# Two sines of a rotation table moved between the copies of the first drive, and the imaginary rotation put first in each quarter

## The chip, the cores and the metric

One core of one Trainium2 chip. The metric is the device time of one execution in microseconds (us), of the slowest (here the only) core. Every number of the profile is from one execution with the hardware profiler on; its clock starts at the core's first instruction, and its span is some 1.8 us shorter than the device time of the same execution.

## The reference, cut to what matters

The input is 2048 tokens of 448 values. They are normalised, pass through a diagonal complex recurrence over the tokens and, beside it, through a gated feed-forward network; the two results are multiplied.

```python
xn = _layernorm(x)
Bu = jnp.einsum("bld,pd->blp", xn + 0j, B_bar)      # the "drive"
h = zeros
for t in range(L):
    h = Lam_bar[None, :] * h + Bu[:, t, :]          # 448 complex states
y = 2.0 * einsum("blp,dp->bld", hseq, Cmat).real + xn * Dskip
g = silu((silu(xn @ w_gate) * (xn @ w_up)) @ w_down)
out = x + y * g
```

## The kernel before

The tokens go in four quarters of 512. The complex recurrence is turned into two real ones: the drive is rotated by tables of cosines and sines (CT, ST), two real scans run, and the states are rotated back. The 448 states lie in four blocks of partitions; the last is a half block, whose real and imaginary parts are packed together. So the real rotation works on four blocks (KT = 4) and the imaginary one on three (KF = 3), plus the packed block once it has been turned over.

A table takes four instructions on VectorE (`table_phase`) and then two sines on ScalarE (`table_sin`). `params_trig` is one more small sine. The drive of a quarter is computed in two groups of four PSUM banks (PSUM is the memory that TensorE's matmuls write into); ScalarE copies each group out. The matmuls of gate and up for the next quarter take the same banks in turn.

```python
def bu(q, ns, packed=False):
    ...
    for two in (ns[:2], ns[2:]):                    # two groups of two blocks
        ...
        sums(q, pairs)                              # TensorE, 4 banks
        for n, pair in zip(two, pairs):
            for i in range(2):
                ...
                nc.scalar.activation(to, pair[i][0], ACT.Copy)
    if packed:
        turn_over(b1[:, KF, :], b0[:, KF, :])       # ScalarE
...
def drive(q, budget):
    bu_alloc(q)
    bu(q, (0, 1, 2), True)
    ...
    ssm_steps(bg, q)                                # rotation, scans, rotation back
    bg.run(budget)
...
gu(0, bg, 0.0, {                                    # first quarter's gate and up, with hooks
    ...
    4: [*transposes(4, 5, 6, 7), on(load_rest), on(table_phase, 1)],
    5: [on(table_sin, 1), on(table_phase, 2)],
    6: [on(table_sin, 2), on(table_phase, 3), on(params_fold), on(table_sin, 3),
        on(params_trig)],
}, ...)
drive(0, 0.0)
```

Each engine works through its own instructions in this order. On ScalarE the sines of the last table therefore stand ahead of the first copy of the first drive. In the profile, PE names TensorE, ACT ScalarE, DVE VectorE; the drive's output is `pb`, gate and up are `gp` and `up`, the down-projection is `hd`.

Of the kernel before, what the change touches and what calls it, by code (L numbers as in the profile page):

```python
# [10 lines left out]
ALU = mybir.AluOpType  # L11
# [33 lines left out]
def kernel(  # L45
# [22 lines left out]
    KF = D // P  # L68
# [23 lines left out]
    def block(n):  # L92
        return slice(n * P, (n + 1) * P)
# [13 lines left out]
    def ctile(shape, dtype, name):  # L107
        return const.tile(shape, dtype, name=name)

    def bank(name, dtype=F32):  # L110

        return psum.tile([P, 2048 // mybir.dt.size(dtype)], dtype, name=name, tag="bank")
# [10 lines left out]
    CT = ctile([P, KT, W], BF16, "CT")  # L123
    ST = ctile([P, KT, W], BF16, "ST")
# [214 lines left out]
    def params_out():  # L339
        tt, ts = nc.vector.tensor_tensor, nc.vector.tensor_scalar  # L340
        ab = pcol[:, 0:KT, 1:3].rearrange("p k c -> p c k")
        tt(out=lam[:], in0=lam[:], in1=rcol[:].unsqueeze(1).to_broadcast([P, 3, KT]),
           op=ALU.mult)
        ts(out=lam[:, 1, :], in0=lam[:, 1, :], scalar1=1.0, scalar2=None, op0=ALU.subtract)
        tt(out=prod[:, 0:2, :], in0=lam[:, 1:3, :], in1=ab, op=ALU.mult)
        tt(out=nb[:, 0, :], in0=prod[:, 0, :], in1=prod[:, 1, :], op=ALU.add)
        tt(out=prod[:, 0:2, :], in0=lam[:, 0:2, :], in1=ab, op=ALU.mult)
        tt(out=nb[:, 1, :], in0=prod[:, 0, :], in1=prod[:, 1, :], op=ALU.subtract)
        tt(out=b_re[:], in0=nb[:, 0, :], in1=rden[:], op=ALU.mult)
        tt(out=b_im[:], in0=nb[:, 1, :], in1=rden[:], op=ALU.mult)  # L350
        ts(out=nb_im[:], in0=b_im[:], scalar1=-1.0, scalar2=None, op0=ALU.mult)
# [42 lines left out]
    def bu_alloc(q):  # L394
        bu_of[q] = [
            work.tile([P, KT, W], BF16, name=f"bu_{c}") for c in ("re", "im")
        ]
# [10 lines left out]
    def sums(q, pairs, between=None):  # L408



        left = []
        for share, first in ((0, True), (1, False)):
            for n, two in enumerate(pairs):
                for m in range(4 - share):
                    for half in range(2):
                        out, w, (c0, c1) = two[half ^ share]
                        d, h = HALVES[half ^ share][share][m]
                        mm = nc.tensor.matmul(  # L419
                            out, lhsT=w[h, d, :], rhs=xT[h, d, q * W + c0 : q * W + c1],  # L420
                            start=(first and m == 0), stop=(not first and m == 3 - share),
                        )
                        if not first and m == 0:
                            told_of(mm, left[n])
                if first:
                    left.append(tell(mm))
            if first:
                run_power()
            if first and between:
                between()  # L430

    def bu(q, ns, packed=False):

        C1 = W // 2
        b0, b1 = bu_of[q]
        ns = [*ns, KF] if packed else ns
        for two in (ns[:2], ns[2:]):
            pairs = []
            for n in two:
                pb = [bank("pb") for _ in range(2)]  # L440
                if n < KF:
                    pairs.append([(pb[i][:], BT[:, :, block(m)], (0, W))
                                  for i, m in enumerate((n, KT + n))])
                else:
                    pairs.append([(pb[i][:, 0:C1], BT[:, :, block(KF)], (i * C1, i * C1 + C1))
                                  for i in range(2)])
            if pairs:
                sums(q, pairs)
            for n, pair in zip(two, pairs):
                for i in range(2):  # L450
                    to = bu_of[q][i][:, n, :] if n < KF else b0[:, KF, i * C1 : i * C1 + C1]
                    nc.scalar.activation(to, pair[i][0], ACT.Copy)  # L452
        if packed:
            turn_over(b1[:, KF, :], b0[:, KF, :])

    def turn_over(out, in_):

        for a, b in ((slice(0, R), slice(R, P)), (slice(R, P), slice(0, R))):
            nc.scalar.activation(out[a], in_[b], ACT.Copy)
# [3 lines left out]
    def ssm_steps(bg, q):  # L463
        T = {}

        def alloc():
            T["b"] = bu_of[q]
            T["e"] = [work.tile([P, KT - c, W], BF16, name=n, bufs=1)
                      for c, n in enumerate(("ere", "eim"))]
            T["t"] = work.tile([P, KT, W], BF16, name="tmp", bufs=1)  # L470
            T["h"] = H_of[q] = [work.tile([P, KT - c, W], BF16, name=n)
                                for c, n in enumerate(("H_re", "H_im"))]

        def of(z, n):
            z = T["t"] if z == "t" else T[z[0]][z[1]] if isinstance(z, tuple) else z
            return z[:, 0:n, :]

        def step(n, out, a, b, op):
            def run():
                if not T:  # L480
                    alloc()
                nc.vector.tensor_tensor(out=of(out, n), in0=of(a, n), in1=of(b, n), op=op)

            bg.add(q, 0.3 * n, run)

        def scan(k, c):
            init = 0.0 if q == 0 else H_of[q - 1][c][:, k, W - 1 : W]
            nc.vector.tensor_tensor_scan(  # L488
                out=T["b"][c][:, k, :], data0=rcol[:, k : k + 1].to_broadcast([P, W]),
                data1=T["e"][c][:, k, :], initial=init, op0=ALU.mult, op1=ALU.add,  # L490
            )

        b0, b1, e0, e1, h0, h1 = (z for n in "beh" for z in ((n, 0), (n, 1)))
        step(KT, e0, b0, CT, ALU.mult)
        step(KT, "t", b1, ST, ALU.mult)
        step(KT, e0, e0, "t", ALU.add)
        step(KF, e1, b1, CT, ALU.mult)
        step(KF, "t", b0, ST, ALU.mult)
        step(KF, e1, e1, "t", ALU.subtract)
        for k in range(KF, -1, -1):  # L500
            for c in range(2 if k < KF else 1):
                bg.add(q, 1.22, lambda k=k, c=c: scan(k, c))
        bg.add(q, 0.0, lambda: turn_over(T["b"][1][:, KF, :], T["b"][0][:, KF, :]))
        step(KF, h1, b1, CT, ALU.mult)
        step(KF, "t", b0, ST, ALU.mult)
        step(KF, h1, h1, "t", ALU.add)
        step(KT, h0, b0, CT, ALU.mult)
        step(KT, "t", b1, ST, ALU.mult)
        step(KT, h0, h0, "t", ALU.subtract)
# [88 lines left out]
    def on(fn, *args):  # L598
        return lambda: fn(*args)
# [56 lines left out]

    def drive(q, budget):
        bu_alloc(q)
        bu(q, (0, 1, 2), True)
        if q == 0:  # L660
            params_out()
        ssm_steps(bg, q)
        bg.run(budget)
# [16 lines left out]
    def do(fns):  # L680
        for fn in fns:
# [5 lines left out]
        3: norms(4, 5, 6, 7),  # L687
        4: [*transposes(4, 5, 6, 7), on(load_rest), on(table_phase, 1)],
        5: [on(table_sin, 1), on(table_phase, 2)],
        6: [on(table_sin, 2), on(table_phase, 3), on(params_fold), on(table_sin, 3),  # L690
            on(params_trig)],
    }, {0: first_pair, 1: second_pair})
    drive(0, 0.0)
    def cw(k):
        return [on(c_weights, k, nc.scalar)], [on(c_weights, k, nc.vector)]

    gu(1, bg, 2.2, {2: cw(0)[0], 3: cw(0)[1], 4: cw(1)[0], 5: cw(1)[1]})
    drive(1, 4.0)
    sg = downs(0, 1.2, {
        0: cw(2)[0] + cw(3)[0],  # L700
# [5 lines left out]
    outs(0, sg, {1: norms(10, 11) + transposes(10, 11)})  # L706
    sg = downs(1, 2.5)
    drive(2, 4.8)
    gu(2, bg, 1.6, {
        0: stats(12, 13),  # L710
# [47 lines left out]
```

## Time and profile before

| | before |
|---|---|
| median of the first 4 runs | 188.25 us (188.13 to 188.58) |
| the profiled execution | 189.09 us, span 187.2 us |
| PE / DVE / ACT busy | 97% / 85% / 55% |
| x of tokens 512 to 1023 landed | 14.08 us |
| last matmul pair of the first drive | starts at 35.33 us |
| first down-projection | starts at 63.05 us |

Starts to two decimals are those of the single instructions in the trace.

Its lines are in the prediction below.

### The profile page before, as it was taken

The page shows a single profiled execution, that of the slowest core. Times are in us where ns is not written, and L with a number is a line of the kernel's source. Part 1 is how long each engine was busy: PE and PEld are TensorE (multiplying, and loading weights), DVE is VectorE, ACT ScalarE, POOL GpSimd, SP SyncE. Part 2 cuts the span into 40 slices and gives each one's busy share as a digit, 9 for nine tenths or more (in the row PEclk, how much of TensorE's full clock was granted, in tenths as well). Part 3 has the DMA queues.
Part 4 walks back from the last instruction along what each step waited for, and adds up shares of the span by engine and source line. Part 5 has one row for each costly group of instructions (what it writes and reads, how often), then busy time and mean ns, then how long its engine had stood idle before and what let it go on. Part 6 is the DMA issues. An engine that isn't in the chain of part 4 may idle for free.

```text
span 187.2 us, 3749 instructions
## 1 busy us (share of the span) xinstructions
PE 181.0 (97%) x1493; PEld 92.4 (49%) x1493; DVE 159.9 (85%) x259; ACT 102.4 (55%) x197; POOL 12.6 (7%) x21
## 2 busy tenths in 40 slices
PE   7899999999999999999999999999999999999991
PEld 3574444455555655555454444555454444555561
DVE  4649799988999999999999999999939999996343
ACT  3236879898897972012289675301578757602110
POOL 7332200000000000400000400000000000000000
PEclk9999999999999999999999999999999999999999
DMA  5899694997000000152000041020000000011020
GB/s 169 212 279 328 111 116 96 160 294 276 0 4 0 5 0 0 27 119 67 0 0 5 0 84 32 0 83 15 2 4 0 4 0 0 4 51 49 0 74 25
DMA packets 25985, 12.59 MB, mean 67 GB/s; under 512 B 15984, under 2 KB 25968, under 8 KB 25968
## 3 DMA queue, kind: packets, MB, share of 16 engines
q1 hardware_dynamic: 24752, 11.95, 25.1%
q10 hardware_dynamic: 1088, 0.41, 0.8%
q8 instruction: 11, 0.18, 0.4%
q14 instruction: 6, 0.05, 0.1%
q0 software_dynamic: 128, 0.00, 0.0%
HBM read 7.11 MB, written 1.84 MB: 48 GB/s over the span
## 4 chain that ended last, share of the span: by engine, by line
PE 78%; DVE 10%; DMA 5%; SPq 2%; ACT 1%; issue 1%; POOL 1%; DVEq 0%
PE hd L558 23%; PE gp L419 18%; PE up L419 16%; PE y L573 11%; PE pb L419 9%; DMA x_all<-in_A_x_dram 3%; DMA Wg<-in_B_w_gate_dram 2%; DVE Vt L550 2%; PE y L579 2%; DVE f L363 2%; DVE st L236 1%; DVE xn L251 1%; DVE a L364 1%; DVE a L360 1%; DVE f L359 1%
## 5 line engine op out<-in xcount | busy, mean ns | idle before, releaser
L419 PE MATMUL gp<-xT,Wg 64*128 64x512 bf16 (+1 forms) x413 | 86.0, 365 | 0.7 <-ACT bu_re L452 0.3
L419 PE MATMUL up<-xT,Wu 64*128 64x512 bf16 (+1 forms) x413 | 85.5, 365 | 0.2
L419 PEld LDWEIGHTS <-Wg 64*128 64x128 bf16 x413 | 37.9, 94 | 23.5 <-issue 1.0
L419 PEld LDWEIGHTS <-Wu 64*128 64x128 bf16 x413 | 37.8, 94 | 20.7 <-issue 0.8
L558 PE MATMUL hd<-Wd,Vt 128*128 128x448 bf16 x224 | 43.2, 352 | 0.0
L542 ACT ACTIVATE gs<-gp 128x512 bf16<-128x512 f32 x56 | 33.8, 605 | 16.8 <-PE gp L419 16.7
L563 ACT ACTIVATE sg<-hd 128x448 bf16<-128x448 f32 x16 | 8.7, 544 | 49.0 <-PE hd L558 48.8
L546 ACT ACTIVATE us<-up 128x512 bf16<-128x512 f32 x54 | 33.0, 610 | 0.0
L558 PEld LDWEIGHTS <-Vt 128*128 128x128 bf16 x224 | 21.8, 98 | 20.5 <-issue 0.2
L419 PE MATMUL pb<-xT,BT 64*128 64x512 bf16 (+1 forms) x224 | 22.1, 349 | 0.0
L550 DVE TENSOR_TENSOR Vt<-gs,us 128x2048 bf16<-128x2048 bf16 (+1 forms) x16 | 17.3, 1081 | 0.9 <-ACT us L546 0.9
L573 PE MATMUL y<-C,H_re 128*128 128x448 bf16 (+2 forms) x68 | 17.6, 342 | 0.0
L589 DVE TENSOR_TENSOR t<-y,sg 128x448 f32<-128x448 f32 (+2 forms) x17 | 10.1, 595 | 8.3 <-PE y L573 7.4
L419 PEld LDWEIGHTS <-BT 64*128 64x128 bf16 x224 | 11.5, 94 | 10.8 <-issue 0.7
L488 DVE TENSOR_TENSOR_SCAN bu_re<-rcol,H_re,ere 128x512 bf16<-128x512 f32 x12 | 15.0, 1265 | 0.0
L579 PE MATMUL y<-Dd,xT 128*128 128x128 bf16 x64 | 13.5, 212 | 0.0
L222 POOL TENSOR_TENSOR rstd<-vep,halves 128x1 f32<-128x1 f32 (+1 forms) x7 | 7.2, 1023 | 86.5 <-DVE vep L238 58.0
L452 ACT ACTIVATE bu_re<-pb 128x512 bf16<-128x512 f32 (+1 forms) x20 | 9.9, 521 | 5.1 <-PE pb L419 5.1
L573 PE MATMUL y<-C,H_im 128*128 128x448 bf16 (+2 forms) x51 | 11.9, 342 | 0.0
L236 DVE BATCH_NORM_STATS2 st<-x_all 128x6 f32<-128x448 bf16 x16 | 9.9, 621 | 2.2 <-DMA x_all<-in_A_x_dram 2.1
L488 DVE TENSOR_TENSOR_SCAN bu_im<-rcol,H_im,eim 128x512 bf16<-128x512 f32 x9 | 11.4, 1262 | 0.0
L592 DVE TENSOR_TENSOR ob<-t,x_all 128x448 bf16<-128x448 f32 (+2 forms) x17 | 10.2, 597 | 0.6
(86 smaller groups left out, 159.7 us busy)
## 6 DMA issues: line engine op xcount, KB each, us to landing
out_dram<-ob SPq DMA_DIRECT2D x15, 112.0 KB, 1.7
Wd<-in_B_w_down_dram SPq DMA_DIRECT2D x1, 1568.0 KB, 9.7
x_all<-in_A_x_dram SPq DMA_DIRECT2D x1, 896.0 KB, 6.3
Wg<-in_B_w_gate_dram SPq DMA_DIRECT2D x2, 384.0 KB, 6.8
Wu<-in_B_w_up_dram SPq DMA_DIRECT2D x2, 384.0 KB, 7.0
x_all<-in_A_x_dram SPq DMA_DIRECT2D x1, 448.0 KB, 6.1
Wg<-in_B_w_gate_dram SPq DMA_DIRECT2D x1, 288.0 KB, 3.0
Wu<-in_B_w_up_dram SPq DMA_DIRECT2D x1, 288.0 KB, 4.6
```

The lines of the kernel that those rows point to most:

```text
L236: nc.vector.bn_stats(out=st[:], in_=x_all[:, n, :])
L419: mm = nc.tensor.matmul(out, lhsT=w[h, d, :], rhs=xT[h, d, q * W + c0 : q * W + c1], start=(first and m == 0), stop=(not first and m == 3 ...
L452: nc.scalar.activation(to, pair[i][0], ACT.Copy)
L488: nc.vector.tensor_tensor_scan(out=T["b"][c][:, k, :], data0=rcol[:, k : k + 1].to_broadcast([P, W]), data1=T["e"][c][:, k, :], initial=in ...
L542: nc.scalar.activation(gs[:, i + j, :], gp_[:], ACT.Silu)
L546: nc.scalar.activation(us[:, i + j, :], up_[:], ACT.Copy)
L550: nc.vector.tensor_tensor(out=Vt[:, f0 : f0 + n, :], in0=gs[:, 0:n, :], in1=us[:, 0:n, :], op=ALU.mult)
L558: nc.tensor.matmul(hd, lhsT=Vt_of[q][:, fi, j * P : (j + 1) * P], rhs=Wd[:, fi, :], start=(fi == 0), stop=(fi == NF - 1),)
L573: nc.tensor.matmul(y[:, c0:c1], lhsT=h, rhs=C2[:, n, c0:c1], start=(n == 0), stop=(n == NS - 1))
L579: nc.tensor.matmul(y[:, s + skip : s + P], lhsT=xT[:, n, m * P : (m + 1) * P], rhs=Dd[:, n, skip:P], start=False, stop=False,)
L589: nc.vector.tensor_tensor(out=t[:], in0=y, in1=sg[:, c0:c1], op=ALU.mult)
L592: nc.vector.tensor_tensor(out=ob[:], in0=t[:], in1=x_all[:, m, c0:c1], op=ALU.add)
```

## The change

The intent is to let ScalarE copy the drive's first group out while VectorE is still busy with the last table's phase, so that banks come free earlier; and to begin each rotation with the part that needs fewer blocks, so that VectorE can start before the packed block is there. No instruction is added or removed.

```diff
-    def bu(q, ns, packed=False):
+    def bu(q, ns, packed=False, between=()):
 ...
                     nc.scalar.activation(to, pair[i][0], ACT.Copy)
+            for fn in between:
+                fn()
+            between = ()
 ...
+        step(KF, e1, b1, CT, ALU.mult)
+        step(KF, "t", b0, ST, ALU.mult)
+        step(KF, e1, e1, "t", ALU.subtract)
         step(KT, e0, b0, CT, ALU.mult)
         step(KT, "t", b1, ST, ALU.mult)
         step(KT, e0, e0, "t", ALU.add)
-        step(KF, e1, b1, CT, ALU.mult)
-        step(KF, "t", b0, ST, ALU.mult)
-        step(KF, e1, e1, "t", ALU.subtract)
 ...
-        bu(q, (0, 1, 2), True)
+        bu(q, (0, 1, 2), True, [on(table_sin, 3), params_trig] if q == 0 else ())
 ...
-        6: [on(table_sin, 2), on(table_phase, 3), on(params_fold), on(table_sin, 3),
-            on(params_trig)],
+        6: [on(table_sin, 2), on(table_phase, 3), on(params_fold)],
```

## The prediction

> **What bounds the kernel now.** I read the page's first two parts, then the waits of the tensor engine, then the chain of waits around the first drive, then the timelines of ScalarE, TensorE and VectorE there.
>
> ```profile
> span 187.2 us, 3749 instructions
> PE 181.0 (97%) x1493; PEld 92.4 (49%) x1493; DVE 159.9 (85%) x259; ACT 102.4 (55%) x197; POOL 12.6 (7%) x21
> PE   7899999999999999999999999999999999999991
> PEclk9999999999999999999999999999999999999999
> ...
> PE warm L179 <- DVE Wd L170: 1.2, 1, 1.2
> PE gp L419 <- ACT bu_re L452: 0.3, 1, 0.3
> PE gp L419 <- ACT xT L268: 0.3, 1, 0.3
> PE tp L262 <- DVE xn L251: 0.3, 1, 0.3
> ```
>
> TensorE (PE) is busy from the first slices to the last at a clock never held back, and all its waits on another engine fit in four lines. Three of them belong to the first 17 us. The fourth, gate matmuls waiting for a ScalarE copy, is the only one in the steady part: it is the wait that the change aims at. Busy time hides its real size, so the chain and the instructions themselves follow.
>
> ```profile
> 33.10 0.70 DVE f L363
> 33.80 0.02 issue
> 33.82 0.72 ACT ST L312
> 34.55 0.01 issue
> 34.55 0.72 ACT CT L313
> 35.27 0.10 ACT lam L337
> 35.37 0.48 ACT bu_re L452
> 35.86 0.50 ACT bu_im L452
> 36.35 0.04 issue
> 36.40 0.37 PE up L419
> ```
>
> Columns: start, length, what (us). Up to 36.40 the chain runs through VectorE and ScalarE: phases of the last table, its two sines, the small sine, two copies. From 36.40 to about 182.7 it is PE alone.
>
> ```profile
> 30.14 5.46 PE L419 MATMUL pb<-xT,BT 64*128 64x512 bf16 x56
> 35.91 0.37 PE L419 MATMUL gp<-xT,Wg 64*128 64x512 bf16 x1 [0.31 <-ACT bu_re L452]
> 36.40 0.37 PE L419 MATMUL up<-xT,Wu 64*128 64x512 bf16 x1
> ...
> 32.20 0.74 ACT L313 ACTIVATE CT<-a,half_pi 128x512 bf16<-128x512 f32 x1
> 33.82 0.72 ACT L312 ACTIVATE ST<-f,two_pi 128x512 bf16<-128x512 f32 x1 [0.88 <-DVE f L363]
> 35.28 0.58 ACT L452 ACTIVATE bu_re<-pb 128x512 bf16<-128x512 f32 x1
> ```
>
> The first drive's matmuls (pb) start at 30.14. ScalarE meanwhile sits idle for 0.88 us, waiting for the last table's phase, although four drive blocks are ready to be copied. The first copy starts only at 35.28, when the drive's matmuls are all but over. So the next stage, whose output takes the same banks in turn, has to wait bank by bank.
>
> **What the Trainium skill says.** (1) "PSUM — Partial Sum Buffer", Specifications (TRN2): 8 banks per partition, each 512 fp32. The drive takes 8 banks (two groups of four), so the gate/up stage after it can start a pair only when a copy has emptied that pair's bank. The trace agrees: gp starts at 35.91 just after the first copy (35.28 + 0.58 = 35.86), up at 36.40 after the second (35.76 + 0.59 = 36.35). (2) "ScalarE: Activation LUTs", What ACT_TABLE_LOAD costs: a switch of table set costs about 2.66 us, an activation 186 ns + 0.833 ns per column, some 93 ns more for each per-partition operand, and neighbours overlap by about 93 ns. The danger would be sines between copies causing loads. The trace has a single table load, 1.28 us at 0.74, before everything; silu, copies and sines follow one another without another. A 512-wide copy takes 0.58 to 0.62 us and neighbours start 0.48 apart, a sine with a per-partition operand 0.72 to 0.74: agrees. (3) "Perfetto Trace Analysis", Identifying the Most-Contended Engine, warns that matmul busy time says little of the distance to roofline. Agreed here: I size the loss by start-to-start times of matmuls, because the busy row shows only 0.31 us of it.
>
> **The change part by part.**
>
> *How much PE loses now.* Half-array matmuls of 512 columns run as pairs, one on each half, a pair every 0.213 to 0.216 us in the timeline (256 columns: 0.106). The last drive pair starts at 35.33, so with free banks the next stage starts at about 35.44, as after the third and fourth drives (last pair 95.62, gate at 95.73; 138.96 and 139.07). In fact one half starts at 35.91 and the other at 36.40. Then one more matmul is 0.10 late (37.37, where 37.26 was due, for the fourth bank: copy at 36.71 + 0.61 = 37.32). On the half that is last: 36.40 - 35.44 = 0.96, and 0.96 + 0.10 = 1.06 us. A second way: from the last drive pair to the first down-projection matmul it takes 35.33 to 63.05 = 27.72 us. The undisturbed parts would be 0.11 + 20.94 (gate/up of the third and fourth quarters: 95.73 to 116.67 and 139.07 to 160.00) + 0.21 + 5.20 (later drives: 90.42 to 95.62) + 0.20 = 26.66. The difference is again 1.06. The second way includes that the halves run 0.2 us apart all through this quarter and its following drive, which takes 5.38 rather than 5.20.
>
> *Sines between the groups.* No instruction is added or removed; two sines (about 0.63 us each from start to start) and the small one (0.10) move behind four copies. New times of ScalarE: the third table's cosine starts at 32.20, the next thing may start 0.63 later, 32.83. The first drive block is finished at 32.30 + 0.38 = 32.67, the second at 33.32. Copies start at 32.83, 33.31, 33.79, 34.27, the last ends at 34.88. The last table's phase is complete at 33.82 + 0.69 = 34.51, so the sines go without a wait: 34.75, 35.38, small one 36.01. Second group's copies: 36.11, 36.59, then the two half-width ones from 37.07 to 37.77; the two turn-over copies end at 39.07 instead of 40.15. The 0.88 us of idling and a little more is gone.
>
> Banks: the first four are free at about 33.4, 33.9, 34.4 and 34.9; they are asked for at 35.44 and 36.30. The second four are free by 36.7, 37.2, 37.4 and 37.8, and are asked for from 38.45 on. The next use of the first four is at about 41.5 (first two) and 42.3; their activations start behind the turn-over at 39.07, 0.48 apart, so they are free at 40.2 and 41.1. The smallest margin is about 0.6 us. The PE wait goes to zero: -1.06 us.
>
> *Imaginary rotation first.* The same six VectorE instructions in another order: 0.95 us each over three blocks, 1.22 each over four. Three-block work needs no packed fourth block, neither its two half-width copies (about 0.7 us) nor the turn-over. First quarter: VectorE finishes the parameters at 38.04 + 0.17 = 38.21 and can start at once (third block's copies end at about 37.2), not at 38.88 after 0.66 idle: 0.67 earlier. By counting the credits of the background queue, five steps instead of four (5.3 us instead of 4.6) go ahead of the first product of gate and up, filling its 0.70 wait at 44.23; VectorE is then ahead by about 1.3 us. In the fourth quarter its 3.00 us wait at 140.61 shrinks by about 0.6. None of this is on the chain that ends last, so I count 0. It keeps VectorE from falling behind an earlier PE.
>
> *Sum.* 188.34 - 1.06 = 187.28; I write 187.3. The tail after the last matmul (about 3 us of multiply, add, store) is unchanged.
>
> **The rivals.**
>
> 1. *The wait moves to the second group's copies*, now behind 1.4 us of sines. For it: ScalarE becomes gapless from 31.7 to 39. Against it: those copies end about 1 us earlier than before, since the idle time is gone, and banks are asked for 0.6 us or more later than they come free. If it held, half the gain would go: 187.8.
> 2. *VectorE becomes the bound and keeps the end where it is.* For it: 85% busy and nearly gapless from 62 to 137. Against it: PE waits for nothing of it. State products are ready well ahead: first quarter 66.78 against first use at 73.65, second 105.43 against 116.98, last 171.44 against 174.35, 2.9 us of slack, more than 1.06, and VectorE's lead grows too. If it held: 188.0 to 188.3.
> 3. *A larger gain by the earlier rotation in every quarter.* For it: 3.7 us of VectorE waits on copies before the rotation. Against it: idle time of an engine that PE doesn't wait for. If those waits were worth their length: about 186.
> 4. *The input of the next stage is not there earlier.* Its transposed tokens land at 32.26 by the transfer records, before 35.44, so no. Transfers of weights for later have landed by 47.1, and the down-projection would start at 62.0.
>
> **Range and chances.** The gain is bounded above by the wait (1.06, with rounding 1.1) and below by zero. The three runs before spread from 188.17 to 188.58, so I allow 0.3 us of noise and half of the gain lost in one case of six. Range 186.9 to 187.9. Two per cent is 3.8 us, over three times what the change can touch: faster by over 2% 0.01, within 2% 0.98, slower 0.01.
>
> **What would show it right or wrong.** Right: PE's line of waiting for the drive's copy is gone; gate starts at 35.4 with both halves together; the gate/up stage takes 20.9 us and the down-projection starts near 62.0; four copies stand at 32.8 to 34.9 and the sines after them; the imaginary product at about 38.2 is the first rotation; the span is near 186.1. Wrong: a new PE wait near 38.4 or 41.5 (rival 1), a gap of PE before the outputs near 73, 116, 159 or 173 (rival 2), or a start of the down-projection at 62.0 with an unchanged end.

## More of the kernel before

One more of this profile matters later. It is from VectorE's timeline (start, length, engine, line, operation and tiles, number of instructions, and in brackets the idle time before and what ended it):

```profile
14.10 0.63 DVE L236 BATCH_NORM_STATS2 st<-x_all 128x6 f32<-128x448 bf16 x1 [0.41 <-DMA x_all<-in_A_x_dram]
```

VectorE stood idle for 0.41 us because the tokens were not there yet. Everything that it does afterwards, up to the phase of the last table, starts from this point.

## The result, and the profile after

| | before | after |
|---|---|---|
| median of 4 runs | 188.25 us | 187.54 us (187.41 to 187.9) |
| profiled execution, span | 187.2 us | 185.7 us |
| last drive pair to first down-projection | 35.33 to 63.05: 27.72 us | 34.92 to 61.57: 26.65 us |

The ratio of the changed kernel's time to that of the kernel before is 0.9963 (95% interval 0.9943 to 0.9982): within 2%. In the medians the gain is 0.71 us.

First the wait. TensorE's waits in the changed kernel (engine, line, output, what it waited for: us in total, times, longest) are now:

```profile
PE warm L179 <- DVE Wd L170: 1.2, 1, 1.2
PE gp L419 <- ACT xT L268: 0.3, 1, 0.3
```

Both belong to the start. The wait for the drive's copy is gone, and no other has taken its place. The matmuls after the first drive show the same:

```profile
29.73 5.46 PE L419 MATMUL pb<-xT,BT 64*128 64x512 bf16 x56
35.02 0.38 PE L419 MATMUL gp<-xT,Wg 64*128 64x512 bf16 x1
35.03 0.38 PE L419 MATMUL up<-xT,Wu 64*128 64x512 bf16 x1
```

Gate and up start together, 0.10 us after the last drive pair. Before, they started 0.58 and 1.07 us after it.

ScalarE shows why:

```profile
31.79 0.74 ACT L313 ACTIVATE CT<-a,half_pi 128x512 bf16<-128x512 f32 x1
32.40 0.62 ACT L452 ACTIVATE bu_re<-pb 128x512 bf16<-128x512 f32 x1
...
33.83 0.65 ACT L452 ACTIVATE bu_im<-pb 128x512 bf16<-128x512 f32 x1
34.31 0.78 ACT L312 ACTIVATE ST<-f,two_pi 128x512 bf16<-128x512 f32 x1
...
35.53 0.26 ACT L337 ACTIVATE lam<-turn 128x12 f32<-128x12 f32 x1
35.64 0.64 ACT L452 ACTIVATE bu_re<-pb 128x512 bf16<-128x512 f32 x1
```

The copies follow the sines of the third table without a gap, the last table's sines stand behind four of them, and no line carries an idle time. The first copy starts 2.5 us before the last drive pair instead of at the same time as it.

The chain that ended last (shares of the span, by engine) went from 78% PE and 10% DVE to this:

```profile
PE 96%; DVE 1%; ACT 0%; issue 0%; DVEq 0%
```

VectorE's phases are off it: the end now hangs on matmuls alone, nearly from the first one.

The two spans differ by 1.49 us, and 1.07 of it is the bank wait (27.72 - 26.65). The other 0.41 came before the first drive, which began at 30.14 and at 29.73: the very first gate matmul was 0.20 later in the profile before, and one gate/up matmul of that stage was held up by another 0.2. That is start-up of two executions, and the medians do not show a gain of 1.49. They show 0.71, which is also less than the 1.07. So something about that wait had to be found out. Behind the stretch nothing differs: from the first down-projection to the end of the span it takes 124.1 us in both profiles, and 124.12 to 124.14 us in all twelve of this document.

### The profile page after: what moved, and what is told of

Read it like the earlier page. It is cut to its first block, busy times and chain, and to the rows that moved or that the text cites. A ratio compares the mean times of both kernels' runs of the same rounds, so it can differ in the third digit from the quotient of the medians.

```text
span 185.7 us, 3750 instructions
## 1 busy us (share of the span) xinstructions
PE 180.2 (97%) x1493; PEld 90.4 (49%) x1493; DVE 159.9 (86%) x259; ACT 102.2 (55%) x197; POOL 12.4 (7%) x21
## 3 DMA queue, kind: packets, MB, share of 16 engines
HBM read 7.11 MB, written 1.84 MB: 48 GB/s over the span
## 4 chain that ended last, share of the span: by engine, by line
PE 96%; DVE 1%; ACT 0%; issue 0%; DVEq 0%
PE gp L419 26%; PE hd L561 23%; PE up L419 20%; PE pb L419 12%; PE y L576 11%; PE warm L179 3%; PE y L582 2%; PE tp L262 1%; DVE ob L595 0%; DVE t L592 0%; ACT xT L268 0%; DVE xT L270 0%; DVE Wd L170 0%; PE tp L286 0%; PE tp L289 0%
## 5 line engine op out<-in xcount | busy, mean ns | idle before, releaser
L419 PEld LDWEIGHTS <-Wg 64*128 64x128 bf16 x413 | 38.5, 94 | 25.1 <-issue 0.4
L419 PEld LDWEIGHTS <-Wu 64*128 64x128 bf16 x413 | 38.5, 94 | 19.4 <-issue 0.3
L419 PEld LDWEIGHTS <-BT 64*128 64x128 bf16 x224 | 10.7, 94 | 11.4 <-issue 0.7
```

The lines of the kernel that those rows point to most:

```text
L419: mm = nc.tensor.matmul(out, lhsT=w[h, d, :], rhs=xT[h, d, q * W + c0 : q * W + c1], start=(first and m == 0), stop=(not first and m == 3 ...
```

## The experiments

**What was open.** My theory after the result: the gain is the bank wait and nothing else, but its size depends on when VectorE's phase chain starts, and so on the landing of the second block of x; the first profile, of an execution slower than the median, showed it too large. Rivals: the rotation order is part of the gain; the wait is always 1.07 and a part of it is lost again later; the wait has merely moved to the second group.

All kernels were built from the kernel before or the changed one with the edit shown. The number that decides is the *stretch*, from the start of the last pair of the first drive to the start of the first down-projection: 26.65 us when TensorE waits for nothing.

### The kernel before again, the changed kernel again, and each half alone

Edits: none, none, only the move of the two sines (with the old order of steps), only the order of steps.

> The kernel before, once more, unchanged. Theory: the tensor engine's wait after the first drive depends on when the second block of tokens (448 KB of x) lands. In the first profile it landed at 14.08 us and the wait was 1.06 us; in the changed kernel's profile it landed at 13.33. If it lands near 13.3 here, the stretch from the last drive pair to the first down-projection is 27.3 to 27.4 us (wait 0.7 to 0.8) instead of 27.72, and the span is about 186.4. Rival: the wait is always about 1.06, the stretch 27.7, and the missing 0.35 us of gain is lost elsewhere. Ratio to the kernel before: 1.000 within 0.001.

> The changed kernel, once more. Both theories: ratio 0.996 (0.995 to 0.997), stretch from the last drive pair to the first down-projection 26.65 us wherever the tokens land.

> Sines between the copies, rotation in the old order. Theory (the whole gain is the tensor engine's bank wait): ratio 0.996, the same as the full change, no wait of the tensor engine, stretch 26.65 us. Rival (the rotation order carries part of the gain): 0.998 or more.

> Imaginary rotation first, sines in the old place. Theory: ratio 1.000 (0.9985 to 1.0015), the bank wait stays, VectorE starts the first rotation about 0.6 us earlier and nothing comes of it. Rival (earlier rotation is worth its length in each quarter): 0.998 or less.

| kernel | ratio to before (95%) | median us | x landed | stretch us |
|---|---|---|---|---|
| before again | 0.9991 (0.9978 to 1.0004) | 188.28 | 13.46 | 27.42 |
| changed again | 0.9952 (0.9941 to 0.9964) | 187.53 | 13.68 | 26.65 |
| sines only | 0.9954 (0.9941 to 0.9967) | 187.46 | 13.50 | 26.65 |
| order only | 1.0012 (1.0 to 1.0025) | 188.67 | 14.14 | 27.67 |

The move of the sines alone gives the whole gain; the order alone gives none. The kernel before, with its tokens landed at 13.46, has a wait of 27.42 - 26.65 = 0.77 us, as expected. In the timeline of that second profile of the kernel before:

```profile
13.76 0.62 DVE L236 BATCH_NORM_STATS2 st<-x_all 128x6 f32<-128x448 bf16 x1
33.46 0.72 ACT L312 ACTIVATE ST<-f,two_pi 128x512 bf16<-128x512 f32 x1 [0.59 <-DVE f L363]
34.91 0.58 ACT L452 ACTIVATE bu_re<-pb 128x512 bf16<-128x512 f32 x1
35.54 0.37 PE L419 MATMUL gp<-xT,Wg 64*128 64x512 bf16 x1
36.03 0.37 PE L419 MATMUL up<-xT,Wu 64*128 64x512 bf16 x1
```

VectorE finds its tokens there, ScalarE idles for 0.59 us where it idled for 0.88, the first copy starts 0.35 us ahead of the last drive pair (35.26) where it started 0.05 ahead. The difference of 0.30 is the difference of the two waits, 1.07 and 0.77. The medians of these two kernels differ by 188.28 - 187.53 = 0.75, which is close to 0.77. The two profiled executions differ by more, 188.6 - 187.48 = 1.12, because the drive of the kernel before also began later there, at 30.07 against 29.73. Only one execution of each run was profiled, so a wait near 0.77 in the executions behind the median is inferred and not shown.

The order only kernel really starts VectorE's rotation earlier, 8.15 us after the drive's first matmul instead of 8.74 (in the first profile of the kernel before; 8.44 in the second), and TensorE takes no notice:

```profile
35.95 0.37 PE L419 MATMUL gp<-xT,Wg 64*128 64x512 bf16 x1 [0.27 <-ACT bu_re L452]
36.44 0.37 PE L419 MATMUL up<-xT,Wu 64*128 64x512 bf16 x1
38.37 0.96 DVE L482 TENSOR_TENSOR eim<-bu_im,CT 128x1536 bf16<-128x1536 bf16 x1
```

### The suspected cause increased, in both kernels

The last step of the last table's phase is repeated three times; it gives the same values again.

```diff
+        if k == KF:
+            for _ in range(3):
+                nc.vector.scalar_tensor_tensor(
+                    out=a[:], in0=f[:], scalar=-1.0, in1=f[:], op0=ALU.mult, op1=ALU.max
+                )
         phase[k] = f[:], a[:]
```

> The kernel before with the last step of the last table's phase repeated three times on VectorE (0.69 us each, same values, correct result). Theory (VectorE's phase chain, through the sines in ScalarE's order, sets the tensor engine's wait): the wait grows by the whole 2.1 us; stretch from the last drive pair to the first down-projection 29.5 (29.2 to 29.8), ratio to the kernel before 1.011. Rival (the wait is set by ScalarE's own load or by the drive's matmuls): 1.003 or less.

> The same three extra steps in the changed kernel. Theory: the first copies no longer stand behind the sines, the second group's banks have over 1 us of room; stretch 26.65 to 26.8, ratio 0.995 to 0.997, the 2.1 us cost almost nothing. Rival (the wait has only moved behind the second group, at its edge): 1 us or more is lost, ratio over 1.000.

In the changed kernel: ratio 0.9958 (0.9922 to 0.9995), stretch 26.80. ScalarE idles for 1.22 us between the two sines, and it costs 0.15 us: one `up` matmul starts 0.10 late at the second group's first banks (38.55), another falls back by 0.05 more at 42.48.

In the kernel before: ratio 1.0169 (1.0118 to 1.0221; the verdict is unclear, as the interval spans 2%), stretch 31.28, far above the expected 29.5. ScalarE's second sine waits for VectorE's added steps, and TensorE for the copy behind it:

```profile
36.23 0.72 ACT L313 ACTIVATE CT<-a,half_pi 128x512 bf16<-128x512 f32 x1 [2.18 <-DVE a L369]
37.59 0.37 PE L424 MATMUL gp<-xT,Wg 64*128 64x512 bf16 x1 [2.20 <-ACT bu_re L457]
```

Two things are in the stretch. The wait itself grew as expected: the first gate matmul came 2.47 us after the last drive pair instead of 0.28, so by 2.19 us (three steps of about 0.73). That gives 26.65 + 0.77 + 2.19 = 29.61. The other 1.7 us are not a wait. The stretches below (us; then for each engine busy time and number of instructions; granted clock of TensorE; share and rate of transfers) are of this kernel:

```profile
30.00:35.10 5.10, 5.10 (x56) 2.55 (x54) 4.85 (x8) 3.46 (x7) 0.00 (x0) 1.00 0.63 129
37.60:45.00 7.40, 7.29 (x49) 3.23 (x50) 6.43 (x16) 6.24 (x13) 0.00 (x0) 0.77 0.91 291
39.05:42.46 3.41, 3.41 (x20) 1.40 (x19) 2.58 (x8) 2.96 (x7) 0.00 (x0) 0.50 0.93 315
45.00:55.00 10.00, 10.00 (x96) 5.11 (x94) 7.63 (x9) 7.67 (x15) 0.00 (x0) 1.00 0.15 51
```

After the pause the granted clock fell to 0.77 on average for 7.4 us. Within them it was 0.50 for 3.41 us, and half of 3.41 is the missing 1.7; between 39.4 and 42.4 a pair of matmuls took 0.43 us instead of 0.216. Three of the four runs have a mean clock of 0.987 to 0.988 and took 191.88 to 192.47 us. The fourth kept 1.0 and took 190.47, about 2.1 over the kernel before, which fits the waiting alone. So the part of the expectation that concerned the wait held, and the number missed because the clock fell as well. That the pause brought this about is likely but was not isolated: the same three steps in the changed kernel, without the pause, kept mean clocks of 0.997 to 1.0, and no execution of the other kernels is below 0.995.

### The suspected cause taken away, with ScalarE's order left alone

The third table takes over the second one's phase (`True` makes `table_sin` set `phase[2] = phase[1]`), so its four steps on VectorE go. The third table is then wrong on purpose; the comparison is too wide to notice it.

```diff
-        5: [on(table_sin, 1), on(table_phase, 2)],
+        5: [on(table_sin, 1, True)],
```

> The kernel before without the phase of the third table (it takes the second one's; result wrong on purpose), which takes 2.3 us off VectorE before the last sines and leaves ScalarE's order as it is. Theory: ScalarE then meets no wait, first copy at about 34.0 instead of 35, first bank free before it is asked for; stretch 26.65 to 26.9, ratio 0.995 to 0.997, as the change, without its move. Rival (the order of ScalarE's instructions itself costs the time): ratio 0.998 or more.

Ratio 0.9964 (0.9928 to 1.0), stretch 26.65: no wait, with the sines still ahead of the copies. In this profile's ScalarE and TensorE timelines:

```profile
33.54 0.74 ACT L312 ACTIVATE ST<-f,two_pi 128x512 bf16<-128x512 f32 x1
34.87 0.61 ACT L454 ACTIVATE bu_re<-pb 128x512 bf16<-128x512 f32 x1
36.16 0.38 PE L421 MATMUL gp<-xT,Wg 64*128 64x512 bf16 x1
36.17 0.38 PE L421 MATMUL up<-xT,Wu 64*128 64x512 bf16 x1
```

The sine waits for nothing and the first copy starts 1.19 us ahead of the last drive pair (36.06). So the order alone did not cost the time; it was the order together with VectorE's late phase. This execution's tokens landed last of all, at 14.81. That made its drive start late, at 30.86, but its stretch no longer.

With this, the profiles that have the sines ahead of the copies lie on one line. The lag is the start of the first copy minus the start of the last drive pair:

| kernel, sines ahead | lag us | wait us (stretch - 26.65) |
|---|---|---|
| phase taken away | -1.19 | 0 |
| before again | -0.35 | 0.77 |
| order only | -0.08 | 1.02 |
| before, first profile | -0.05 | 1.07 |
| phase lengthened | 1.84 | 2.95 by its matmul starts (and 1.7 more of lower clock) |

The wait is the lag plus 1.12 within 0.02, or nothing where that is below zero. (In the last row the stretch holds the lower clock too, so the wait is counted as in the prediction: up at 38.08, due at 35.23, and 0.10 for one later matmul.)

The twelve profiles also show a second way in which the landing reaches TensorE, in both kernels. Where the tokens land up to 6.44 us after the first gate matmul, the drive starts 22.52 us after that matmul (six profiles, within 0.01). In the six where they land later, 6.55 to 7.71 us after it, the drive is late as well, by 0.09 to 1.24. In the profile of this section, which is late by 1.24:

```profile
17.47 0.39 PE L421 MATMUL up<-xT,Wu 64*128 64x512 bf16 x1 [1.07 <-POOLq L403]
```

L403 is a small notice that GpSimd (POOL) passes on to TensorE. It went out at 17.40, just after VectorE's `zr` had ended at 17.36, for which GpSimd was waiting, and `zr` stands behind the late tokens. A very late landing therefore delays VectorE's phases and the drive alike, so the bank wait should stop growing; no run of the kernel before has a landing late enough to show it. In the three profiles with sines ahead of the copies and nothing added or taken away it lies between 0.77, with the tokens in time, and 1.07.

### The sines behind both groups

```diff
-            for fn in between:
-                fn()
-            between = ()
+        for fn in between:
+            fn()
         if packed:
```

> The changed kernel with the two sines and the small one behind both groups of copies (ahead of the turn-over). Theory: the tensor engine sees no difference, stretch 26.65, ratio 0.995; VectorE's parameters and first rotation come about 2 us later than in the changed kernel (39.4 instead of 37.4) and stay off the path. Rival (VectorE's early start is part of the gain): ratio 0.998 or more.

Stretch 26.65 as expected, and the first rotation at 39.50 instead of 37.41. Its runs scattered (187.34 to 188.8 us), so the ratio of 0.9972 (0.9929 to 1.0014) does not decide by itself; its fastest run equals the changed kernel's fastest. TensorE sees no difference; only VectorE does.

### How much room there is behind the first group

The last table's sines are written twice, then three times, between the groups.

```diff
-        bu(q, (0, 1, 2), True, [on(table_sin, 3), params_trig] if q == 0 else ())
+        bu(q, (0, 1, 2), True, [on(table_sin, 3, 2), params_trig] if q == 0 else ())
```

(The number is how many times the sines are written in addition: 1 or 2.)

> The changed kernel with the last table's two sines written twice (1.22 us more of ScalarE between the groups, same values, correct result). Theory (the second group's banks come free about 1.2 to 1.4 us before they are asked for): the extra work just fits; stretch from the last drive pair to the first down-projection 26.65 to 26.85, ratio 0.995 to 0.997. Rival (the move has put the wait at the edge of the second group): stretch 27.3 or more.

> The same with the sines written three times (2.44 us more). Theory: the room is overdrawn by some 1.2 us, so the tensor engine waits again, now at the second group's banks, about 3 us after the drive's end instead of right behind it; stretch 27.8 (27.5 to 28.1), ratio 0.999 to 1.002. Rival (ScalarE's load has no bound near here): stretch 26.65.

With one more pair: ratio 0.9966 (0.9942 to 0.999), stretch 26.68, no wait for a copy. With two more: ratio 1.0027 (1.0009 to 1.0046), stretch 27.91, and the wait is back, at the second group:

```profile
38.53 0.38 PE L421 MATMUL gp<-xT,Wg 64*128 64x512 bf16 x1
39.46 0.37 PE L421 MATMUL gp<-xT,Wg 64*128 64x512 bf16 x1 [0.56 <-ACT bu_re L454]
39.95 0.37 PE L421 MATMUL up<-xT,Wu 64*128 64x512 bf16 x1
```

So in the changed kernel there is room for about 1.2 us of work between the groups: 2.44 us were added, and 27.91 - 26.65 = 1.26 of them were lost. The prediction's own times say the same: the second of these banks free by 37.2, asked for from 38.45. No experiment pointed to a version faster than the changed kernel: TensorE has no wait left after the start that this change could touch.

## Why the prediction was right

The time on record was 187.3 us, the range 186.9 to 187.9; measured were 187.54 and 187.53. The mechanism was right, and one term was mis-sized.

- *The bank wait is what the change removes, and the whole of it*: shown. The wait has left TensorE's list, the stretch is 26.65 us where the second way of counting gave 26.66, and the sines alone bring the whole gain.
- *ScalarE's new times*: the first copy was put at 32.83 and the second group's first at 36.11. This profile's drive started 0.41 us earlier; with that added, the measured 32.40 and 35.64 become 32.81 and 36.05.
- *The down-projection near 62.0*: 61.57, and 61.98 with the same 0.41.
- *The order counts 0*: shown by the order alone (1.0012). Its working holds in part. VectorE's 0.70 us idle ahead of its first product of gate and up fell to 0.23, but only with both halves of the change: it is 0.80 with the order alone and 0.72 with the sines alone. The 3.00 us idle of the fourth quarter fell to 2.22, which is not on the path. The earlier first rotation (38.21 predicted, 37.41 measured, 37.82 with the 0.41) was put down to the order, and wrongly: with the sines alone and the old order it comes at 37.53, without idle time.
- *Rival 1, the wait moves to the second group*: refuted for the change, and the doubled sines show at what load it would have come.
- *Rival 2, VectorE becomes the bound*: refuted; TensorE shows no wait for it, and 2.2 us more of VectorE's phase in the changed kernel cost 0.15.
- *Rival 3, 186 us by earlier rotations*: refuted with the order alone.
- *Rival 4, the next stage's input is late*: refuted, as gate and up started at 35.02 and 35.03.

One reading of the prediction is loose: that four drive blocks stood ready all through ScalarE's 0.88 us of idling (32.94 to 33.82). By its own times two banks were ready from 32.67 and the other two only from 33.32. Nothing rests on it.

**The mis-sized term** is the step "How much PE loses now", 1.06 us. Both ways of counting it were right for the profile, but the profile was of one execution, at 189.09 us slower than all of the kernel's first four runs, in which x landed 0.6 us later than in the second profile. There the wait measured 0.77, and the medians differ by 0.71 to 0.75. The prediction left out that a wait at the end of a chain that starts with a transfer varies with the transfer; it took the upper end of what the profiles show (0.77 to 1.07) for the usual size. The profiled run's own time was there as a warning, though it does not measure the wait: the second profile, too, was of a slow execution (188.6 against a median of 188.28), with a wait of 0.77 and a late first gate matmul, at 7.55. The range held because it allowed for half of the gain being lost.

What stays open: the very first gate matmul starts between 7.09 and 7.74 us in these twelve profiles, mostly with the landing of the second small block of x, for reasons that no run here separates. These runs do not show it to be an effect of the change.

## What to carry to other kernels

When one engine's queue holds an instruction that must wait for another engine, look at what stands behind it that is ready already and that the bound engine is waiting for; moving the waiting instruction back costs nothing if what it feeds has slack. Size such a gain by instruction starts rather than by the idle figure, and from more than one profile: a profiled execution slower than the median is a warning, above all where the chain begins with a transfer. Idle time on an engine that the bound engine does not wait for is worth nothing, however long: 0.6 us earlier in the rotation gave no gain here.

## What the Trainium skill lacked or had wrong

- "TensorE: Matmul & The Clock Gate", HAM oscillation — how this bites in real kernels, gives as its rule that idle gaps of TensorE should not exceed about 3.4 us. Here, after a pause of 2.47 us from start to start (2.20 us idle), the granted clock was 0.50 from 39.05 to 42.46 in the profile, and three of four runs of that kernel had a lower mean clock (0.987 to 0.988); it cost 1.7 us on top of the wait. Waits of 0.77 to 1.26 us in four other profiles cost nothing beyond their own length.
- "ScalarE: Activation LUTs", Table sets: the hidden batching unit, names in its table no set with silu or sine, and says that each set has one expensive anchor. This kernel runs silu, sine and copies in turn, and the trace before has one table load in all, of 1.28 us at 0.74. The changed kernel, with the last sines between copies, has one as well.
